# Block-sorted attention and a routed expert layer: a fixed order for the attention phase, and another access pattern where mixed k and v leave PSUM

## The chip, the core and the metric

One core of a Trainium2 chip runs the whole program in one launch. Time is device microseconds of one execution. The kernel before takes 630.01 us (median of 3 runs, 629.17 to 630.42). Its engines are named as in the profile: PE (TensorE, matmuls), PEld (its weight loads), DVE (VectorE), ACT (ScalarE), POOL (GpSimd) and SP (SyncE, which issues DMAs). POOL and ACT issue DMAs too.

## What is computed

There are 4 x 8 = 32 attention heads with a sequence of 768 rows, cut into 8 blocks of 96, and a head size of 64. A small matrix P (8 x 8 for each head) is normalised five times; it mixes the blocks of k and of v; each block of q then attends to the mixed block at its own place. The result, 3072 rows of 512, goes through a router, which sends each row to one of 8 experts.

```python
P = sort_net
for _ in range(5):
    P = np.exp(P - np.max(P, axis=-1, keepdims=True))
    P = P / (np.sum(P, axis=-1, keepdims=True) + 1e-09)
    P = P / (np.sum(P, axis=-2, keepdims=True) + 1e-09)
k_sorted = np.einsum('bhij,bhjcd->bhicd', P, k_b)
v_sorted = np.einsum('bhij,bhjcd->bhicd', P, v_b)
scores = scale * np.matmul(q_b, k_sb.transpose(0, 1, 2, 4, 3))
attn = softmax(scores)               # over the last axis
x = np.matmul(attn, v_sb)            # then rows of 512
e_idx = np.argmax(x @ w_gate + modality_bias[modality_id], axis=1)
out[mask] = gate_w * (np.maximum(x[mask] @ w1[e], 0.0) @ w2[e])   # for each expert e
```

## The kernel before

The heads are handled in two groups of 16 (`g` = 0, 1). The stages follow one another like this.

- Loads. `load_k(g)` brings k of a group in 6 pieces of 256 KB into a small buffer (`k_raw`, two of them) and spreads each into `k_il`, a zero-filled array in which the two halves of the partitions take alternate columns. `load_v(g)` brings v in one DMA of 1.5 MB into `v_in`. `load_q(g, hq)` brings two heads' q and rearranges it on VectorE into `q_il`. All three issue DMAs from GpSimd's queue, which works in order, as all the queues do.
- Normalisation. Five rounds (lines 119 to 131) of Exp on ScalarE and six short VectorE operations, each waiting for the one before. Lines 133 to 159 make the mixing matrices `bd_k` and `bd_v` out of the result.
- Mixing. A group has 28 jobs, 12 of `sort_k` and 16 of `sort_v`. A job is 8 or 4 matmuls into one PSUM bank (`mipsum`, two slots) and one copy of 512 values per partition from there to SBUF, with conversion to bf16. The copy of `sort_k` goes to `kTb`, where neighbouring values of the copy land 192 bytes apart; that of `sort_v` goes to `v_sb`, where they land 130 bytes apart. Group 0's jobs run before the first unit, alternating between VectorE and ScalarE.
- Units. 32 units, one head of a group and half of its blocks each: `trans_q` (6 transposes on TensorE, one copy on VectorE; only in the first half of a group), `scores` (8 matmuls), `expo` (one Exp on ScalarE), `av` (8 matmuls, then two reciprocals and two multiplications on VectorE, which write `xb`). From u = 2 to 15 two jobs of group 1 are written into each unit, one for each of the two engines. After every eighth unit, SyncE issues 12 DMAs of 64 KB that write `xb` to `x_scratch` in DRAM. There is one `xb`, so the first write of the next block waits for them.
- Between mixing and the units stands the set-up of the router: small constants, a load of `w_gate`, and a DMA that fills `sidx_scratch` with 3968 records of 8 bytes out of a tile (`dummy_t`) that VectorE clears.
- Router. 24 tiles of 128 rows are read back from `x_scratch` (ScalarE's queue), transposed, multiplied with `w_gate`; each ends in a small write to `cnt_scratch` on GpSimd's queue. After the last one `cnt` is read back, a serial chain computes where each row goes, and 24 indirect DMAs scatter the row numbers.
- Experts. 31 slots of 128 rows, each gathered, multiplied with w1 and w2 of one expert, and scattered to the output. The weights of all 8 experts lie in `w_all`, 8192 columns of each partition for one expert; `kTb`, `v_in`, `k_il` and the transposed q occupy the columns of experts 3 to 7 during attention, so those weights can be loaded only when these are done with. `load_weights(e)` is two DMAs of 1 MB each on GpSimd's queue.

The order of the instructions on each engine is not the program's. A scheduler places them by its own cost estimates and by program order as a priority, and it moves what is independent a long way: the set-up of the router runs inside the first 25 us, and weight loads are issued from 27 us on, wherever their columns are free.

Of the kernel before, what the change touches and what calls it, by code (L numbers as in the profile page):

```python
# [17 lines left out]
def kernel(  # L18
# [67 lines left out]
    nc.vector.memset(k_il[0:64, :, 1], 0.0)
    nc.vector.memset(k_il[64:128, :, 0], 0.0)
    load_k(0)
    load_v(0)
    q_tiles = {}  # L90
# [424 lines left out]
```

## Time and profile before

| | us |
|---|---|
| median of 3 runs | 630.01 |
| the profiled execution | 628.43 |
| its span, from the first to the last instruction | 626.3 |
| start to the first copy of a mixed chunk | 50.0 |
| mixing of group 0 | 47.4 |
| units with jobs of group 1 between them | 67.6 |
| the other units, with the writes of x, to the router's first transposes | 68 |
| router | 57.2 |
| routing chain and scatter of the row numbers | 121.8 |
| experts | 214.3 |

[...] Over the span PE is busy 44%, DVE 42%, ACT 31% and POOL 22%: no engine is near full over the whole, so each stage has to be read by itself. In the rows further down, a group of instructions shows its line, engine, operation, the tiles it writes and reads, shapes and count, and behind the bar its busy time, the mean length of one in ns, and the idle time of its engine just before it with what ended it. In a timeline a row begins with its start and its length in us; the square bracket holds the idle time before it and what ended that.

### The profile page before, as it was taken

To read this page: it belongs to the slowest core of one execution; us is meant where nothing else is said; L and a number is where in the kernel's file an instruction comes from. 1 tells how busy PE (TensorE), PEld (TensorE's weight loads), DVE (VectorE), ACT (ScalarE), POOL (GpSimd) and SP (SyncE) were. 2 spreads that over 40 slices of the span, in tenths; PEclk is the share of its full clock that TensorE was granted. 3 is DMA by queue.
4 is the path that set the end of the run, shared out by engine and by line. 5 is a ranking of instruction groups with operands and counts; after the bars stand their busy time and mean duration, and the time that the engine had idled before them with its cause. 6 is when DMAs were issued, how large, how long until landed. Compare 5 with 4: busy or idle time off the path is not lost.

```text
span 626.3 us, 6878 instructions
## 1 busy us (share of the span) xinstructions
PE 277.0 (44%) x2026; PEld 157.8 (25%) x2044; DVE 261.8 (42%) x769; ACT 192.7 (31%) x431; POOL 137.3 (22%) x180
## 2 busy tenths in 40 slices
PE   0002327653754406551000000068787886787775
PEld 0002225542532203331000000023333333333332
DVE  4438888878743506553000000023444343433342
ACT  0006775787332205551000000023333332333222
POOL 5311102110000101222222222122332332223222
PEclk9999999999999999999999999999999998999999
DMA  7999858793826593210000000011121121211210
GB/s 141 119 121 204 140 83 152 117 196 58 136 51 112 83 201 81 59 40 1 7 0 0 0 0 0 0 42 52 51 69 58 50 76 35 68 51 52 46 17 10
DMA packets 41337, 43.56 MB, mean 70 GB/s; under 512 B 14396, under 2 KB 32869, under 8 KB 41046
## 3 DMA queue, kind: packets, MB, share of 16 engines
q0 software_dynamic: 25184, 36.72, 31.6%
q1 hardware_dynamic: 12662, 3.26, 3.4%
q10 hardware_dynamic: 3456, 3.15, 2.2%
q8 instruction: 18, 0.29, 0.2%
q14 instruction: 17, 0.14, 0.1%
HBM read 59.83 MB, written 11.33 MB: 114 GB/s over the span
## 4 chain that ended last, share of the span: by engine, by line
DMA 29%; PE 27%; issue 16%; DVE 15%; ACT 8%; POOL 3%; SPq 1%; POOLq 0%; DVEq 0%; ACTq 0%
DMA sidx_scratch<-rg_all,dest_i_all 12%; PE h_p L462 8%; PE y_p L477 7%; DMA x_scratch<-xb 4%; PE hT_p L473 3%; ACT v_sb L175 3%; DVE v_sb L175 3%; DVE y_sb L481 3%; DMA x_t<-x_scratch,idxg 3%; DVE w_all L168 3%; DMA k_raw<-in_k_dram 3%; DMA q_in<-in_q_dram 2%; ACT w_all L168 2%; DMA out_dram<-y_sb,idxg 2%; PE va L173 2%
## 5 line engine op out<-in xcount | busy, mean ns | idle before, releaser
L456 PE MATMUL xT_p<-ident,x_t 128*128 128x128 bf16 x124 | 21.3, 221 | 141.2 <-DMA x_t<-x_scratch,idxg 123.4
L477 PE MATMUL y_p<-w_all,hT 128*128 x237 | 73.2, 379 | 0.6 <-ACT hT L474 0.6
L457 ACT COPY xT<-xT_p 128x128 bf16<-128x128 bf16 x62 | 16.5, 266 | 167.4 <-PE xT_p L456 167.4
L462 PE MATMUL h_p<-w_all,xT 128*128 x241 | 60.4, 391 | 9.9 <-issue 9.6
L450 POOL DMA_INDIRECT x_t<-x_scratch,idxg x31 | 30.5, 983 | 133.1 <-PE h_p L462 50.9
L457 DVE COPY xT<-xT_p 128x128 bf16<-128x128 bf16 x62 | 11.5, 217 | 111.3 <-PE xT_p L456 111.2
L473 PE MATMUL hT_p<-ident,h_sb 128*128 128x128 bf16 x248 | 49.6, 221 | 10.7 <-DVE hT L474 9.6
L474 DVE COPY hT<-hT_p 128x128 bf16<-128x128 bf16 x124 | 27.9, 225 | 46.6 <-PE hT_p L473 42.0
L456 PEld LDWEIGHTS <-x_t 128*128 128x128 bf16 x124 | 9.8, 97 | 144.1 <-DMA x_t<-x_scratch,idxg 127.0
L175 DVE CAST v_sb<-va 96x512 bf16<-96x512 f32 x16 | 39.1, 2445 | 10.2 <-PE va L173 10.1
L175 ACT CAST v_sb<-va 96x512 bf16<-96x512 f32 x16 | 39.3, 2454 | 12.5 <-PE va L173 12.5
L474 ACT COPY hT<-hT_p 128x128 bf16<-128x128 bf16 x124 | 32.8, 264 | 29.8 <-PE hT_p L473 26.1
L219 ACT ACTIVATE attnT<-sc 96x768 bf16<-96x768 f32 x32 | 26.8, 841 | 48.9 <-PE op L232 39.1
L467 DVE TENSOR_SCALAR h_sb<-h_p 128x512 bf16<-128x512 f32 x31 | 21.4, 692 | 47.5 <-PE h_p L462 47.5
L434 POOL DMA_INDIRECT sidx_scratch<-rg_all,dest_i_all x24 | 23.4, 974 | 75.7 <-DMA sidx_scratch<-rg_all,dest_i_all 71.3
L469 ACT ACTIVATE h_sb<-h_p 128x512 bf16<-128x512 f32 x31 | 18.5, 597 | 63.8 <-PE h_p L462 58.5
L482 POOL DMA_INDIRECT out_dram<-y_sb,idxg x31 | 31.4, 1014 | 25.9 <-DVE xT L457 13.2
L462 PEld LDWEIGHTS <-xT 128*128 128x128 bf16 x248 | 24.7, 99 | 46.3 <-issue 25.7
L168 ACT CAST w_all<-ka 128x512 bf16<-128x512 f32 x12 | 32.5, 2712 | 8.3 <-PE ka L166 8.3
L477 PEld LDWEIGHTS <-hT 128*128 128x128 bf16 x248 | 23.9, 96 | 44.0 <-issue 16.5
L481 DVE TENSOR_SCALAR y_sb<-y_p,idxg 128x512 f32<-128x512 f32 x31 | 23.3, 751 | 27.3 <-PE y_p L477 26.4
L236 DVE TENSOR_TENSOR xb<-op,rs 96x256 bf16<-96x256 f32 x64 | 26.0, 417 | 18.5 <-DMA x_scratch<-xb 16.9
(126 smaller groups left out, 450.4 us busy)
## 6 DMA issues: line engine op xcount, KB each, us to landing
w_all<-in_moe_w_dram POOLq DMA_DIRECT2D x16, 1024.0 KB, 12.2
k_raw<-in_k_dram POOLq DMA_DIRECT2D x12, 256.0 KB, 7.7
w_all<-in_v_dram POOLq DMA_DIRECT2D x2, 1536.0 KB
q_in<-in_q_dram POOLq DMA_DIRECT2D x16, 192.0 KB, 7.5
x_scratch<-xb SPq DMA_DIRECT2D x48, 64.0 KB, 6.1
x_t<-x_scratch ACTq DMA_DIRECT2D x24, 128.0 KB, 2.4
idxg<-sidx_scratch SPq DMA_DIRECT2D x31, 1.0 KB, 1.7
x_t<-x_scratch,idxg POOLq DMA_INDIRECT x31
```

The lines of the kernel that those rows point to most:

```text
L168: (nc.scalar.copy if act else nc.vector.tensor_copy)(dst, acc)
L175: (nc.scalar.copy if act else nc.vector.tensor_copy)(dst, acc[0:BLK])
L219: nc.scalar.activation(attnT[u % 3][:, 0:8 * BLK].rearrange("p (r f) -> p r f", r=2), sc_tiles.pop(u)[0:BLK, :, 0:4 * BLK], ACT.Exp, scale ...
L450: nc.gpsimd.indirect_dma_start(out=x_t, out_offset=None, in_=x_dram, in_offset=bass.IndirectOffsetOnAxis(ap=idx[:, :1], axis=0))
L456: nc.tensor.transpose(xT_p, x_t[:, c * 128:(c + 1) * 128], ident)
L457: (nc.scalar.copy if c % 2 else nc.vector.tensor_copy)(xT[:, c], xT_p)
L462: nc.tensor.matmul(h_p, xT[:, c], w_all[:, bass.ds(e_sv * WCOL + c * F + half * 512, 512)], start=(c == 0), stop=(c == 3))
L473: nc.tensor.transpose(hT_p, h_sb[:, fc * 128:(fc + 1) * 128], ident)
L474: (nc.scalar.copy if fc % 2 else nc.vector.tensor_copy)(hT[:, fc], hT_p)
L477: nc.tensor.matmul(y_p, hT[:, fc], w_all[:, bass.ds(e_sv * WCOL + 4 * F + fc * Dm, Dm)], start=(fc == 0), stop=(fc == 7))
L481: nc.vector.tensor_scalar(y_sb, y_p, gate_t[:, 0:1], None, ALU.mult)
L482: nc.gpsimd.indirect_dma_start(out=out, out_offset=bass.IndirectOffsetOnAxis(ap=idx[:, :1], axis=0), in_=y_sb, in_offset=None, bounds_chec ...
```

## The change

- From the loads to the last unit everything stands inside `tc.manual_schedule()`: each engine executes its instructions in the order in which the program writes them. The program's order is rewritten for that. The normalisation starts behind one memset, with the spreads of k put into its rounds 2 to 4; mixing of group 0 follows; then the set-up of the router; then the units, in each of which `expo(u)`, `scores(u + 1)`, `prep_q(u + 2)`, two jobs and `av(u)` follow one another.
- The copies of mixed chunks walk the chunk the other way round: the source in PSUM is read with a stride of 256 bytes (k) or 512 bytes (v), and the destination in SBUF is written in runs of 8 values (16 bytes) or 4 values (8 bytes). `v_sb` has rows of 72 values, not 65.
- All jobs of group 1 copy on ScalarE; those of group 0 still alternate.
- k of a group comes in 3 DMAs of 512 KB, straight into the space of `v_sb[1]`; one half of the partitions is spread by VectorE, the other by GpSimd. Some memsets move to GpSimd.
- `xb` lies in the columns of expert 2, one for each half of a group. Therefore the weights of experts 2 to 7 are loaded behind attention; those of experts 0 and 1 at u = 14 and 19 (before: 0, 1 and 2 at u = 14, 18 and 22).

```diff
...
-    KCH = 6
+    KCH = 3
-    def load_k(g):
-        for kc in range(KCH):
-            raw = apool.tile([128, KCW * D], BF16, tag="k_raw", name=f"k_raw{g}_{kc}", bufs=2)
-            nc.gpsimd.dma_start(out=raw, in_=k_src[g * 128:(g + 1) * 128, kc * KCW * D:(kc + 1) * KCW * D])
-            rv = raw.rearrange("p (c d) -> p c d", d=D)
-            for par in range(2):
-                rows = slice(par * 64, (par + 1) * 64)
-                nc.vector.tensor_copy(k_il[rows, kc * KCW:(kc + 1) * KCW, par], rv[rows])
...
-    apool = ph1.enter_context(tc.tile_pool(name="apool", bufs=3))
+    apool = ph1.enter_context(tc.tile_pool(name="apool", bufs=2))
...
+    order = ExitStack()
+    order.enter_context(tc.manual_schedule())
...
+    v_sb = [a1.tile([128, 128, VW], BF16, tag=f"v_sb{gg}", name=f"v_sb{gg}") for gg in range(2)]
+    k_raw = v_sb[1].rearrange("p x d -> p (x d)")[:, 0:BLK * D]
...
+    def load_k(g):
+        for kc in range(KCH):
+            cs = slice(kc * KCW * D, (kc + 1) * KCW * D)
+            nc.gpsimd.dma_start(out=k_raw[:, cs], in_=k_src[g * 128:(g + 1) * 128, cs])
+
+    def spread_k(kc, par):
+        rows = slice(par * 64, (par + 1) * 64)
+        cs = slice(kc * KCW * D, (kc + 1) * KCW * D)
+        eng = nc.gpsimd if par else nc.vector
+        eng.tensor_copy(k_il[rows, kc * KCW:(kc + 1) * KCW, par],
+                        k_raw[rows, cs].rearrange("p (c d) -> p c d", d=D))
...
+    def spread_q(g, hq):
+        t = q_raw.pop((g, hq))
+        il = apool.tile([128, 2, 6, 2, D], BF16, tag="q_il", name=f"q_il{g}_{hq}")
         for z in range(2):
             nc.vector.tensor_copy(il[:, z], t[:, :, z].rearrange("p r (t d) -> p t r d", d=D))
         q_tiles[g, hq] = il
...
+    nc.vector.memset(k_il[0:64, :, 1], 0.0)
+    make_identity(nc, ident)
+    load_k(0)
+    load_v(0)
     load_q(0, 0)
     load_q(0, 1)
-
-    nc.vector.memset(v_in[:, BLK * D:128 * D], 0.0)
-    v_sb = [a1.tile([128, 128, D + 1], BF16, tag=f"v_sb{gg}", name=f"v_sb{gg}") for gg in range(2)]
-    for gg in range(2):
-        nc.gpsimd.memset(v_sb[gg][:, :, D:D + 1], 1.0)
-    attnT = [a1.tile([96, 8 * BLK + 32], BF16, tag=f"attnT{z}", name=f"attnT{z}") for z in range(3)]
+    nc.gpsimd.memset(k_il[64:128, :, 0], 0.0)
+    nc.gpsimd.memset(v_in[:, BLK * D:128 * D], 0.0)
+    for kc in range(KCH):
+        spread_k(kc, 1)
+    nc.gpsimd.memset(v_sb[0][:, :, D:D + 1], 1.0)
     for z in range(3):
         nc.gpsimd.memset(attnT[z][:, 8 * BLK:], 0.0)
...
     for it in range(5):
         if it == 0:
             nc.vector.tensor_reduce(red, P_t, AX.X, ALU.max)
             nc.vector.tensor_tensor(P_t, P_t, red.broadcast_to([BH, NB, NB]), ALU.subtract)
         nc.scalar.activation(P_t, P_t, ACT.Exp)
+        if it == 0:
+            nc.vector.tensor_reduce(jmask, id3s, AX.X, ALU.add)
+        elif it == 1:
+            nc.vector.tensor_reduce(bmask, id3, AX.X, ALU.add)
+            for g in range(2):
+                nc.vector.tensor_copy(sel[g], ident[0:BH, g * 16:(g + 1) * 16].broadcast_to([BH, 16, NB]))
+        else:
+            spread_k(it - 2, 0)
         nc.vector.tensor_reduce(red, P_t, AX.X, ALU.add)
         nc.vector.reciprocal(red, red)
         nc.vector.tensor_tensor(P_t, P_t, red.broadcast_to([BH, NB, NB]), ALU.mult)
...
+    make_bd(0)
...
-        dst = kTb[g].rearrange("p (x c) -> p c x", c=BLK)[:, ch * 8:(ch + 1) * 8]
-        (nc.scalar.copy if act else nc.vector.tensor_copy)(dst, acc)
+        src = acc.rearrange("p z x -> p x z")
+        dst = kTb[g].rearrange("p (x c) -> p x c", c=BLK)[:, :, ch * 8:(ch + 1) * 8]
+        (nc.scalar.copy if act else nc.vector.tensor_copy)(dst, src)
...
-        dst = v_sb[g].rearrange("p x d -> p d x")[0:BLK, ch * 4:(ch + 1) * 4]
-        (nc.scalar.copy if act else nc.vector.tensor_copy)(dst, acc[0:BLK])
...
+        src = acc[0:BLK].rearrange("p z x -> p x z")
+        dst = v_sb[g][0:BLK, :, ch * 4:(ch + 1) * 4]
+        (nc.scalar.copy if act else nc.vector.tensor_copy)(dst, src)
...
     for n, (f, g, ch) in enumerate(sort_jobs[0]):
         f(g, ch, n % 2)
+        if n == 11:
+            load_k(1)
+            make_bd(1)
+    load_v(1)
+    load_q(0, 2)
+    load_q(0, 3)
...
-            x_tiles[g, hf] = apool.tile([BLK, 2, 4, H, D], BF16, tag="xb", name=f"xb{g}_{hf}", bufs=1)
+            x0 = 2 * WCOL + hf * 8 * Dm
+            x_tiles[g, hf] = w_all[0:BLK, x0:x0 + 8 * Dm].rearrange("p (r i h d) -> p r i h d", r=2, i=4, h=H)
...
-    WLOAD = {14: 0, 18: 1, 22: 2}
+    WLOAD = {14: 0, 19: 1}
...
-    load_q(0, 2)
-    load_q(0, 3)
-    trans_q(0, 0)
+    def prep_q(u):
+        if u < 32 and (u // 8) % 2 == 0:
+            if u % 2 == 0:
+                spread_q(u // 16, (u % 8) // 2)
+            trans_q(u // 16, u % 8)
+
+    prep_q(0)
+    prep_q(1)
     scores(0)
     pend = list(sort_jobs[1])
     for u in range(32):
-        if u == 0:
-            load_k(1)
-            load_v(1)
+        if u < 3:
+            spread_k(u, 1)
+            spread_k(u, 0)
+        if u == 3:
+            nc.gpsimd.memset(v_sb[1][:, :, D:D + 1], 1.0)
         if 9 <= u <= 12:
             load_q(1, u - 9)
         if u in WLOAD:
             load_weights(WLOAD[u])
         expo(u)
-        n = u + 1
-        if n < 32:
-            if (n // 8) % 2 == 0:
-                trans_q(n // 16, n % 8)
-            scores(n)
-        av(u)
-        if u >= 2 and u < 16:
+        if u + 1 < 32:
+            scores(u + 1)
+        prep_q(u + 2)
+        if u >= 2:
             for z in range(2):
                 if pend:
                     f, g, ch = pend.pop(0)
-                    f(g, ch, z)
+                    f(g, ch, 1)
+        av(u)
+    order.close()
     ph1.close()
-    for e in range(3, E):
+    for e in range(2, E):
         load_weights(e)
```

## Rows read from the trace of the kernel before

**Rows 1.** Busy time by stage: us, PE, PEld, DVE, ACT, POOL (instructions); PEclk; DMA share, GB/s
```profile
0.00:50.00 50.00, 0.90 (x15) 0.84 (x16) 21.98 (x68) 2.56 (x6) 16.72 (x35) 1.00 0.99 132
50.00:97.40 47.40, 14.58 (x159) 12.45 (x157) 40.75 (x27) 35.95 (x14) 5.45 (x9) 1.00 0.80 132
97.40:165.00 67.60, 39.49 (x444) 31.59 (x442) 55.13 (x80) 44.37 (x27) 10.63 (x14) 1.00 0.81 137
```

**Rows 2.** Chain that ended last, first 50 us: start us, us, what
```profile
24.73 15.69 DMA k_raw<-in_k_dram
```

**Rows 3.** Timeline of the start: start us, us, engine, line, operation, tiles, idle before
```profile
0.25 0.10 POOL L499 MEMSET const-float32-0.0<- 128x1 f32 x1 [0.25 <-issue]
7.13 0.30 POOL masks.py:197 MEMSET ident<- 128x128 bf16 x1
7.63 2.07 DVE L71 COPY w_all<-k_raw 64x1024 bf16<-64x1024 bf16 x4 [0.27 <-DMA k_raw<-in_k_dram]
46.17 0.26 ACT L123 ACTIVATE P_t<-P_t 32x64 f32<-32x64 f32 x1 [1.50 <-DVE P_t L131]
49.12 0.31 DVE L157 TENSOR_TENSOR bdk<-bdv 128x64 bf16<-128x64 bf16 x2
```

**Rows 4.** Groups by line and form, 0 to 300 us: busy us, mean ns, idle
```profile
L175 DVE CAST v_sb<-va 96x512 bf16<-96x512 f32 x16 | 39.1, 2445 | 10.2 <-PE va L173 10.1
L168 ACT CAST w_all<-ka 128x512 bf16<-128x512 f32 x12 | 32.5, 2712 | 8.3 <-PE ka L166 8.3
L236 DVE TENSOR_TENSOR xb<-op,rs 96x256 bf16<-96x256 f32 x64 | 26.0, 417 | 18.5 <-DMA x_scratch<-xb 16.9
L127 DVE TENSOR_REDUCE red<-P_t 32x8 f32<-32x64 f32 x5 | 1.3, 253 | 0.2
L124 DVE TENSOR_REDUCE red<-P_t 32x8 f32<-32x64 f32 x5 | 1.0, 207 | 1.3 <-ACT P_t L123 1.3
```

**Rows 5.** Costliest groups of the page: busy us, mean ns, idle before
```profile
L467 DVE TENSOR_SCALAR h_sb<-h_p 128x512 bf16<-128x512 f32 x31 | 21.4, 692 | 47.5 <-PE h_p L462 47.5
L469 ACT ACTIVATE h_sb<-h_p 128x512 bf16<-128x512 f32 x31 | 18.5, 597 | 63.8 <-PE h_p L462 58.5
```

**Rows 6.** Timeline, TensorE in the first mixing stage
```profile
52.77 1.01 PE L166 MATMUL ka<-bdk,w_all 128*128 128x64 bf16 x16 [2.38 <-DVE w_all L168]
```

**Rows 7.** Busy time, as rows 1, around the 8-byte fill and behind it
```profile
24.00:30.00 6.00, 0.00 (x0) 0.00 (x0) 3.39 (x13) 0.26 (x1) 2.57 (x4) 1.00 0.69 28
40.00:60.00 20.00, 3.32 (x50) 2.83 (x50) 16.77 (x39) 8.92 (x6) 4.71 (x7) 1.00 1.15 205
```

**Rows 8.** DMA issues, whole span: count, KB, median us to landing
```profile
sidx_scratch<-dummy_t SPq DMA_DIRECT2D x1, 31.0 KB, 16.2
```

**Rows 9.** Timeline of the unit loop, TensorE, then ScalarE late in it
```profile
98.25 0.50 PE L213 MATMUL sc<-w_all 64*128 64x96 bf16 x8
98.69 0.82 PE L194 MATMUL tq<-ident,q_il 128*128 128x128 bf16 x6
99.88 0.62 PE L232 MATMUL op<-v_sb,attnT 96*128 96x65 bf16 x8
...
174.72 0.81 ACT L219 ACTIVATE attnT<-sc 96x768 bf16<-96x768 f32 x1 [0.87 <-PE op L232]
176.35 0.81 ACT L219 ACTIVATE attnT<-sc 96x768 bf16<-96x768 f32 x1 [0.83 <-PE op L232]
```

**Rows 10.** Timeline of the issues of x_scratch writes, blocks 2 and 4
```profile
174.25 6.22 SPq L244 DMA_DIRECT2D x_scratch<-xb  x12
...
215.49 8.74 SPq L244 DMA_DIRECT2D x_scratch<-xb  x12
```

**Rows 11.** Chain that ended last: the router's first reload
```profile
230.44 2.68 DMA x_t<-x_scratch
```

**Rows 12.** Timeline, GpSimd at the end of the router
```profile
287.97 0.50 POOL L367 DMA_DIRECT2D cnt_scratch<-cnt_sb  x1 [1.38 <-ACT cnt_sb L366]
290.19 0.53 POOL L370 DMA_DIRECT2D cnt<-cnt_scratch  x1 [1.72 <-DMA cnt_scratch<-cnt_sb]
```

More of the change, by code (lines that the diff above doesn't have):

```diff
@@ L82, with load_v @@
     mipsum = ph1.enter_context(tc.psum_pool(name="mipsum", bufs=2))
+    order = ExitStack()
+    order.enter_context(tc.manual_schedule())
+    v_sb = [a1.tile([128, 128, VW], BF16, tag=f"v_sb{gg}", name=f"v_sb{gg}") for gg in range(2)]
+    k_raw = v_sb[1].rearrange("p x d -> p (x d)")[:, 0:BLK * D]
+    attnT = [a1.tile([96, 8 * BLK + 32], BF16, tag=f"attnT{z}", name=f"attnT{z}") for z in range(3)]
+    ident = singles.tile([128, 128], BF16)
     P_t = singles.tile([BH, NB, NB], FP32)
     nc.sync.dma_start(out=P_t, in_=sort_net.rearrange("b h i j -> (b h) i j"))
[L86 to L90, printed above, removed]
+    def load_k(g):
[8 more added lines that the diff above has]
+                        k_raw[rows, cs].rearrange("p (c d) -> p c d", d=D))
+    def load_v(g):
+        nc.gpsimd.dma_start(out=v_in[:, 0:BLK * D], in_=v_src[g * 128:(g + 1) * 128])
+    q_raw, q_tiles = {}, {}
     def load_q(g, hq):
-        t = apool.tile([128, 2, 2, 6 * D], BF16, tag="q_in", name=f"q_in{g}_{hq}", bufs=2)
+        t = apool.tile([128, 2, 2, 6 * D], BF16, tag="q_in", name=f"q_in{g}_{hq}")
         for par in range(2):
@@ L100, in load_q @@
         q_tiles[g, hq] = il
+    nc.vector.memset(k_il[0:64, :, 1], 0.0)
+    make_identity(nc, ident)
+    load_k(0)
+    load_v(0)
     load_q(0, 0)
     load_q(0, 1)
[L105 to L109 removed]
+    nc.gpsimd.memset(k_il[64:128, :, 0], 0.0)
[3 more added lines that the diff above has]
+    nc.gpsimd.memset(v_sb[0][:, :, D:D + 1], 1.0)
     for z in range(3):
         nc.gpsimd.memset(attnT[z][:, 8 * BLK:], 0.0)
[L112 to L113 removed]
+    jmask = singles.tile([128, NB], FP32)
+    bmask = singles.tile([128, 16], FP32)
+    sel = [singles.tile([BH, 16, NB], BF16, tag=f"sel{g}", name=f"sel{g}") for g in range(2)]
     red = singles.tile([BH, NB], FP32)
@@ L131, with make_bd @@
         nc.vector.tensor_tensor(P_bf if it == 4 else P_t, P_t, colb, ALU.mult)
-    id3 = ident.rearrange("p (a j) -> p a j", j=NB)
-    id3s = bass.AP(tensor=ident.tensor, offset=ident.offset,
-                   ap=[ident.ap[0], [1, NB], [NB, 16]])
-    jmask = singles.tile([128, NB], FP32)
-    nc.vector.tensor_reduce(jmask, id3s, AX.X, ALU.add)
-    bmask = singles.tile([128, 16], FP32)
-    nc.vector.tensor_reduce(bmask, id3, AX.X, ALU.add)
     bd_v, bd_k = [], []
-    for g in range(2):
-        sel = singles.tile([BH, 16, NB], BF16, tag=f"sel{g}", name=f"sel{g}")
-        nc.vector.tensor_copy(sel, ident[0:BH, g * 16:(g + 1) * 16].broadcast_to([BH, 16, NB]))
+    def make_bd(g):
         rep = mipsum.tile([128, NB, NB], FP32, tag="mi", name=f"rep{g}")
-        nc.tensor.matmul(rep.rearrange("p a b -> p (a b)"), sel.rearrange("p a b -> p (a b)"),
+        nc.tensor.matmul(rep.rearrange("p a b -> p (a b)"), sel[g].rearrange("p a b -> p (a b)"),
                          P_bf.rearrange("p a b -> p (a b)"), start=True, stop=True)
@@ L173, in sort_v @@
             nc.tensor.matmul(acc[:, z], v_cols[:, ch * 4 + z], bd_v[g], start=True, stop=True)
-        dst = v_sb[g].rearrange("p x d -> p d x")[0:BLK, ch * 4:(ch + 1) * 4]
-        (nc.scalar.copy if act else nc.vector.tensor_copy)(dst, acc[0:BLK])
-    sort_jobs = []
-    for g in range(2):
-        jobs = [(sort_k, g, ch) for ch in range(12)] + [(sort_v, g, ch) for ch in range(16)]
-        sort_jobs.append(jobs)
+        src = acc[0:BLK].rearrange("p z x -> p x z")
+        dst = v_sb[g][0:BLK, :, ch * 4:(ch + 1) * 4]
+        (nc.scalar.copy if act else nc.vector.tensor_copy)(dst, src)
+    sort_jobs = [[(sort_k, g, ch) for ch in range(12)] + [(sort_v, g, ch) for ch in range(16)]
+                 for g in range(2)]
     for n, (f, g, ch) in enumerate(sort_jobs[0]):
         f(g, ch, n % 2)
+        if n == 11:
[4 more added lines that the diff above has]
+    load_q(0, 3)
     x_tiles = {}
```

12 lines of the change are left out of this document (6 added, 6 removed).

## Prediction

> **What bounds the kernel now.** I read the busy time by stage first [rows 1], then the chain of waits of each stage, then the groups by line. In no stage of attention is TensorE full: from 50.0 to 97.4 us it works 14.6 us of 47.4 while VectorE and ScalarE are busy 40.8 and 36.0, and from 97.4 to 165 VectorE works 55.1 of 67.6. What fills them is one kind of instruction, the copy of a mixed k or v chunk out of PSUM: 2.71 us for k, 2.45 us for v [rows 4], though a dense copy of the same 512 values takes 0.69 us on VectorE and 0.60 us on ScalarE [rows 5]. The first 50 us are another matter: the chain ends in DMAs, the longest a k piece of 15.7 us [rows 2], and the normalisation of sort_net waits on VectorE behind the copies of k. Later VectorE waits 16.9 us in all before line 236 for writes that still read the only xb [rows 4]. The router, the serial scatter and the experts come after the last write, and nothing in the diff touches them: they move with what precedes them.
>
> **The working, in the profile's own time** (span 626.3 us, execution 628.4 us; the median of the three runs is 630.0, so 1.6 more). I put the changed kernel's milestones on the trace's clock.
>
> *Head.* VectorE now does one memset, and the five normalisation rounds are interleaved with only three spreads. A round takes 0.26 + 1.50 = 1.76 us [rows 3]. Two quarter-megabyte k pieces were spread by 9.7 us [rows 3]; at 205 GB/s [rows 7] the remaining 1.05 MB of the first group needs 5.1 us more, so the third spread can end about 15 and, with the last round and 1.4 us for the mixing matrix, mixing could start near 18 instead of 49.4 [rows 3]. GpSimd may be later: after its issues (some 7 us) it clears 6144 and 2048 elements and copies 2048 for the first third. No GpSimd copy is in the trace. The nearest rows are its memsets: 0.10 us for 1 element, 0.30 for 128 [rows 3], 1.56 ns for each further element, so 9.6 + 3.2 + 3.3 us and a start at 23; with 2.3 ns (0.30 / 128) it is 31, with 4-byte words in the memsets 17. I take 23, as a contiguous copy is nearest to that memset; its other two thirds, 3.3 us each, keep ahead of TensorE. [...]
>
> *One eviction, E.* The new copy writes runs of 8 (k) or 4 (v) values and reads PSUM with a jump at every value. Floor: dense, 0.69 and 0.60 us. A jump at every read is in the trace only in SBUF: line 127 against line 124, 253 - 207 = 46 ns on 64 values, 0.72 ns each [rows 4]; on 512 values that is 0.37 us, so 1.06. If each write run costs what a lone value costs now (2.71 us less 0.69, over 512: 3.9 ns), 64 or 128 runs add 0.25 or 0.5, so 1.6 at most in this reckoning. A gain below the floor is excluded, as no dense copy of this size is faster. I take 1.0, nearest to the jumping read. The upper end stays unknown, since no row reads PSUM so; it can lie at today's 2.45 to 2.71 or over.
>
> *Mixing group 0.* Two PSUM slots; a pair of jobs lasts E plus about 0.68 us (TensorE needs 1.01 us for 16 matmuls, two jobs, and is released by the copy [rows 6]; 2.71 + 0.68 is today's period). 14 pairs x 1.68 = 23.5, plus 1.5 for the second matrix now in the middle: 23 + 25 = 48. Today 97.4.
>
> *The first units and a new stall.* Through prep_q(0), prep_q(1) and the small memsets the first expo starts at 52, and u = 0 and 1 take 5.5 with their spreads: at 57.5 the program order asks for q(0,2). GpSimd issues its load only behind load_v(1), which waits for the last mixing matmul. Right then SyncE issues the fill of sidx_scratch, whose zero tile VectorE writes in its new place after mixing. That one DMA of 8-byte records took 16.2 us to land [rows 8], and in its first six microseconds the DMA engines moved 28 GB/s against 205 later [rows 7]; the k piece of [rows 2] was its victim. So I put 13 us of block behind 49, then 1.57 MB of v and 0.39 MB of q at 205 GB/s, 9.6 us: q(0,2) at 72. TensorE and VectorE stand still for 14 us, because trans_q and spread_q head their queues with everything behind. The cost may be 0 if the transfers share, 16 if they don't at all.
>
> *Units.* TensorE per unit: scores 0.50, transposes 0.82, k job 0.5, av 0.62 [rows 6, 9]. With two jobs it needs 2.2 to 2.9 us. ScalarE now takes both evictions: 0.81 + 2 x 1.0 + 0.3 for gaps, 3.1. In-order coupling considered, 3.2, and 3.9 with transposes: 8 x 3.2 + 6 x 3.9 = 49 for u = 2 to 15. Units 16 to 21 have transposes alone, 2.4 each; the last ten keep the period of 1.63 [rows 9], taken 1.6: 30.4. Two xb in expert 2's columns remove the waits for line 236's writes. Last av: 72 + 49 + 30 = 151.
>
> *What is late next.* Writes of the last block: 12 issues take 6.2 us in a quiet block and 8.7 beside weights [rows 10], so x is out after 8: 159, today 230. The router took from 230.4 to 288.0 [rows 11, 12], which gives 217. But the change loads only experts 0 and 1 inside attention; 12 transfers of 1.05 MB start when xb is out, 12.6 / 205 = 61 us, plus some 10 for the router's 3.1 MB sharing the engines, and the 24 small cnt writes stand behind them in the same GpSimd queue: 159 + 70 + 2 = 231. That is the later. Today the reload of cnt is issued at 290.2 [rows 12]: 59 us earlier. All behind it shifts: 628.4 - 59 = 569; I say **569 us**. If loads of free columns (experts 6, 7) are moved up into attention, up to 14 us less.
>
> **Rivals.** (a) *The blocks do not bite*: the fill shares, and weights move up. Then 57.5 + 49 + 30 + 8 = 144.5 and the router's 57.5 decide: cnt at 204.5, 86 earlier, 542 us. For it: beside weights the issue of the x writes only stretched from 6.2 to 8.7 us [rows 10]. Against: the first six microseconds of the fill [rows 7]. (b) *Eviction gains only half*, E = 1.8: mixing ends at 59, q at 83 (fill 60, block and transfers 23), units 14 x 4.7 = 66, then 30, 8 and 72: 259, 31 earlier, 597 us. ScalarE is then the bound, as it has all of group 1. (c) *The change does not do what it says*, E stays near 2.6: the same sums give 71, 94.5, 183, 213, 221 and 293, hence 631 us, no change, since the better head pays only for ScalarE's doubled load and the late weights. (d) *Strided PSUM reads cost as much as scattered writes do now*: 3.9 ns for each of 512 values on top of a dense copy and of the 8-byte runs, E = 3.4. Mixing ends at 82, q at 105.5, units 14 x 7.9 = 111, reload at 327: 664 us, slower. It decides from E = 2.55, where 42 us per microsecond of E (14 pairs and 28 evictions on ScalarE) have eaten the 59. Against it: the jumping SBUF read costs 0.72 ns, not 3.9.
>
> [...]
>
> **How the numbers follow.** The forecast has 0.50 and its own range is 552 to 582 (E from 0.7 to 1.3, head 17 to 31). (a) 0.20, (b) 0.18, (c) 0.04, (d) 0.05; 0.03 for another stall of the fixed order that eats everything, counted as slower. So faster 0.88, same 0.02 and slower 0.10, with (c) halved between the last two. A measurement here tells 0.2% from no change. The range reaches to (a) and (b): 538 to 604.
>
> **What would show it.** Copies at lines of sort_k and sort_v near 1.0 us; P_bf by 18 and the first mixing matmul by 18 to 31; spread_q of the third pair waiting on a q DMA with the fill in flight; ScalarE, not VectorE, densest in u = 2 to 15; no wait before the first xb write of a block; weights landing after the last router tile and the cnt reload waiting for them; an unchanged length from that reload to the end (336 us). Wrong it would be if eviction is over 2 us, or if the fixed order waits for a DMA I have not placed.

## The result, and the profile after

The changed kernel takes 555.64 us (median of 4 runs, 555.13 to 558.68) where the kernel before, on the same chip, takes 630.21: a ratio of 0.883 [0.880, 0.886]. The profiled execution of after has a span of 553.4 us, before 626.3. The forecast of 569 is 13 us too high and inside its own range of 552 to 582; several of its steps missed by more than that, with both signs.

| Milestone on the trace's clock, us | before | predicted | after |
|---|---|---|---|
| first mixing matmul | 49.4 | 23 | 23.1 |
| mixing of group 0 ends | 97.4 | 48 | 43.1 |
| q(0,2) is there | no such wait | 72 | 57.4 |
| units 2 to 15 done | – | 121 | 90 |
| last division by the row sum | 215.6 | 151 | 122.3 |
| last x write landed | 230.1 | 159 | 144.0 |
| reload of cnt issued | 290.2 | 231 | 216.9 |
| end of the span | 626.3 | 567 | 553.4 |

Attention ends 93 us earlier, but only 73 reach the end: the way from the last division to the reload of cnt grew from 74.6 to 94.6 us.

The first view is the busy time by stage, as [rows 1]: stretch, length, PE, PEld, DVE, ACT, POOL, granted clock, DMA share, GB/s.

```profile
0.00:23.00 23.00, 0.21 (x1) 0.21 (x2) 19.25 (x45) 2.56 (x6) 22.09 (x27) 1.00 0.83 160
23.00:43.00 20.00, 14.37 (x161) 12.49 (x160) 10.67 (x23) 8.14 (x14) 0.46 (x2) 1.00 0.49 93
58.00:90.00 32.00, 26.68 (x405) 23.02 (x404) 18.81 (x63) 23.61 (x40) 7.54 (x10) 0.97 1.21 168
90.00:122.00 32.00, 22.40 (x294) 16.90 (x292) 23.27 (x78) 13.28 (x17) 8.91 (x12) 0.50 1.19 220
122.00:145.00 23.00, 0.12 (x2) 0.12 (x3) 1.05 (x5) 0.00 (x0) 2.06 (x4) 0.50 1.18 231
```

Mixing of group 0 fills 20 us with the matmuls that took 47.4 before. From 122 to 145 next to nothing is computed, while the DMA engines move 231 GB/s. Of the 20 us that are lost behind attention, 5 lie there (17.6 us from the last division to the router's first transposes before, 22.7 after) and 15 in the router (57.0 and 71.9 us).

The groups by line of 23 to 122 us, as [rows 4] (busy us, mean ns, idle before):

```profile
L196 ACT CAST v_sb<-va 96x512 bf16<-96x512 f32 x24 | 13.9, 625 | 9.1 <-PE va L193 9.1
L188 ACT CAST w_all<-ka 128x512 bf16<-128x512 f32 x18 | 10.3, 586 | 23.9 <-PE ka L185 23.7
L196 DVE CAST v_sb<-va 96x512 bf16<-96x512 f32 x8 | 5.5, 686 | 4.8 <-PE va L193 4.8
L188 DVE CAST w_all<-ka 128x512 bf16<-128x512 f32 x6 | 4.2, 692 | 4.1 <-PE ka L185 4.1
L261 DVE TENSOR_TENSOR w_all<-op,rs 96x256 bf16<-96x256 f32 x63 | 26.5, 421 | 2.3
```

The copies out of PSUM went from 2712 and 2445 ns to 0.59 to 0.69 us, the floor of [rows 5] and not above it; and the write to xb (last row) waits for no DMA any more.

The timeline, by contrast, shows where after waits (start us, us, what, idle before and who ended it): behind mixing for q, before the router for the modality ids, in the router for cnt.

```profile
57.42 0.63 DVE L110 COPY q_il<-q_in 128x768 bf16<-128x768 bf16 x2 [4.30 <-DMA q_in<-in_q_dram]
57.84 0.82 PE L218 MATMUL tq<-ident,q_il 128*128 128x128 bf16 x6 [6.79 <-DVE q_il L110]
106.05 0.82 PE L218 MATMUL tq<-ident,q_il 128*128 128x128 bf16 x6 [4.77 <-DVE q_il L110]
144.56 0.22 DVE L357 CAST mod<-modraw 24x128 bf16<-24x128 int32 x1 [21.35 <-DMA modraw<-in_moe_modality_id_dram]
170.75 0.15 ACT L397 COPY cnt_sb<-cnt_p 1x8 f32<-1x8 f32 x1 [7.99 <-DMA cnt_scratch<-cnt_sb]
216.85 0.53 POOL L401 DMA_DIRECT2D cnt<-cnt_scratch  x1 [1.35 <-DMA cnt_scratch<-cnt_sb]
```

The last row answers [rows 12]. From it to the end are 336.5 us, before 336.1.

### The profile page after: what moved, and what is told of

It reads as the page before. It is cut to its first block, busy times and chain, and to the rows that moved or that the text cites. A ratio compares the mean times of both kernels' runs of the same rounds, so it can differ in the third digit from the quotient of the medians.

```text
span 553.4 us, 6871 instructions
## 1 busy us (share of the span) xinstructions
PE 268.7 (49%) x2044; PEld 153.5 (28%) x2044; DVE 199.5 (36%) x735; ACT 143.7 (26%) x445; POOL 153.7 (28%) x182
## 4 chain that ended last, share of the span: by engine, by line
DMA 31%; PE 30%; issue 20%; DVE 12%; POOL 4%; ACT 2%; POOLq 0%; SPq 0%; ACTq 0%; DVEq 0%
DMA sidx_scratch<-rg_all,dest_i_all 14%; PE h_p L493 10%; PE y_p L508 9%; DMA q_in<-in_q_dram 4%; PE hT_p L504 4%; DVE y_sb L512 3%; DMA x_t<-x_scratch,idxg 3%; DMA out_dram<-y_sb,idxg 2%; POOL cnt_scratch L398 2%; DMA x_t<-x_scratch 2%; PE ka L185 2%; PE xT_p L487 1%; DMA v_sb<-in_k_dram 1%; PE va L193 1%; DVE w_all L261 1%
## 5 line engine op out<-in xcount | busy, mean ns | idle before, releaser
L487 PE MATMUL xT_p<-ident,x_t 128*128 128x128 bf16 x124 | 21.2, 221 | 139.8 <-DMA x_t<-x_scratch,idxg 121.9
L508 PE MATMUL y_p<-w_all,hT 128*128 x248 | 75.2, 376 | 0.0
L493 PE MATMUL h_p<-w_all,xT 128*128 x248 | 63.3, 401 | 8.9 <-issue 8.7
L504 PE MATMUL hT_p<-ident,h_sb 128*128 128x128 bf16 x248 | 49.4, 220 | 10.3 <-DVE hT L505 9.6
L465 POOL DMA_INDIRECT sidx_scratch<-rg_all,dest_i_all x24 | 23.3, 973 | 77.1 <-DMA sidx_scratch<-rg_all,dest_i_all 72.9
L498 DVE TENSOR_SCALAR h_sb<-h_p 128x512 bf16<-128x512 f32 x31 | 21.4, 692 | 48.4 <-PE h_p L493 46.8
L371 PE MATMUL xT_p<-ident,x_t 128*128 128x128 bf16 x96 | 19.9, 278 | 27.5 <-ACT xT L372 14.6
L512 DVE TENSOR_SCALAR y_sb<-y_p,idxg 128x512 f32<-128x512 f32 x31 | 23.3, 751 | 27.2 <-PE y_p L508 27.2
L398 POOL DMA_DIRECT2D cnt_scratch<-cnt_sb x24 | 12.1, 504 | 58.0 <-ACT cnt_sb L397 41.0
L261 DVE TENSOR_TENSOR w_all<-op,rs 96x256 bf16<-96x256 f32 x64 | 26.9, 421 | 2.3
L504 PEld LDWEIGHTS <-h_sb 128*128 128x128 bf16 x248 | 20.6, 97 | 15.5 <-DVE h_sb L498 14.4
## 6 DMA issues: line engine op xcount, KB each, us to landing
w_all<-in_v_dram POOLq DMA_DIRECT2D x2, 1536.0 KB, 14.6
```

The lines of the kernel that those rows point to most:

```text
L261: nc.vector.tensor_tensor(xb[:, par, :, h], op[0:BLK, :, 0:D], rs.broadcast_to([BLK, 4, D]), ALU.mult)
L465: nc.gpsimd.indirect_dma_start(out=sidx_dram, out_offset=bass.IndirectOffsetOnAxis(ap=dest_i_all[:, t:t + 1], axis=0), in_=rg_all[:, t], i ...
L487: nc.tensor.transpose(xT_p, x_t[:, c * 128:(c + 1) * 128], ident)
L493: nc.tensor.matmul(h_p, xT[:, c], w_all[:, bass.ds(e_sv * WCOL + c * F + half * 512, 512)], start=(c == 0), stop=(c == 3))
L504: nc.tensor.transpose(hT_p, h_sb[:, fc * 128:(fc + 1) * 128], ident)
L508: nc.tensor.matmul(y_p, hT[:, fc], w_all[:, bass.ds(e_sv * WCOL + 4 * F + fc * Dm, Dm)], start=(fc == 0), stop=(fc == 7))
```

## Experiments

The kernel before took 632.6, 630.8, 631.1 and 630.5 us beside the four groups of runs, so kernels are compared by their ratio to it.

**The order alone**: after, with the copies that write single values; the order, the loads and the second `xb` stay.

```diff
-        src = acc.rearrange("p z x -> p x z")
-        dst = kTb[g].rearrange("p (x c) -> p x c", c=BLK)[:, :, ch * 8:(ch + 1) * 8]
...
+        dst = kTb[g].rearrange("p (x c) -> p c x", c=BLK)[:, ch * 8:(ch + 1) * 8]
...
```

(v likewise.)

> The changed kernel with one part undone: the copies of mixed k and v write lone values to SBUF again (dense PSUM reads); order, loads and xb stay. Theory 1 (the new copy carries the gain, and the fixed order pays only because the copy is short): a copy is back at 2.45 to 2.71 us, group 0's mixing takes 14 x 3.3 = 46 us instead of 20, and in u = 2 to 15 ScalarE, which holds both copies of a unit, needs 0.8 + 2 x 2.6 = 6 us a unit, 85 us instead of 32; the reload of cnt moves from 217 to about 290 and the time is 620 to 640, like the kernel before. Theory 2 (the order carries at least half of the gain): 555 to 595.

Measured 626.1 us, 0.991 [0.988, 0.993]: theory 1. The groups and the stage show why the order is worth so little by itself:

```profile
L194 ACT CAST v_sb<-va 96x512 bf16<-96x512 f32 x24 | 56.5, 2507 | 7.0 <-PE va L192 6.9
L187 ACT CAST w_all<-ka 128x512 bf16<-128x512 f32 x18 | 48.3, 2806 | 18.8 <-PE ka L185 18.6
98.00:192.00 94.00, 47.72 (x586) 36.80 (x582) 37.80 (x128) 75.95 (x51) 13.58 (x17) 1.00 0.71 125
```

Mixing starts at 23.1, 26 us earlier, but ScalarE now evicts all of group 1, at 2.5 to 2.8 us each, and is busy 76 of 94 us; last division at 191.6, reload of cnt at 286.1. Rival (c) was this case (E near 2.6, reload 293, 631 us), so its total was good to 1 per cent.

**The copy alone**: before, with the new copies and the wider rows of v that they need.

```diff
+        src = acc.rearrange("p z x -> p x z")
...
-        dst = kTb[g].rearrange("p (x c) -> p c x", c=BLK)[:, ch * 8:(ch + 1) * 8]
...
+        dst = kTb[g].rearrange("p (x c) -> p x c", c=BLK)[:, :, ch * 8:(ch + 1) * 8]
...
```

> The kernel before with one part of the change alone: the copies read PSUM with a stride and write runs of 8 or 4 values (v_sb in rows of 72); the scheduler's order stays. Theory 1 (the copy is what bounded mixing): group 0's mixing falls from 47 to some 20 us and the 14 units with two jobs from 4.6 to about 2.7 us each, together 50 us less by the first write of block 2; the first 50 us, with their DMA waits, and the waits for the one xb stay; weights that came earlier with slack now come late and give some back: 570 to 590. Theory 2 (the scheduler's order has DMA waits that take the place of the copies): over 600.

Measured 587.7 us, 0.930 [0.927, 0.932]: theory 1. Mixing still starts at 49.7, but the stage of [rows 1] that it fills has TensorE busy 31.3 us in place of 14.6:

```profile
L177 ACT CAST v_sb<-va 96x512 bf16<-96x512 f32 x16 | 9.4, 588 | 15.5 <-PE va L174 15.5
50.00:97.40 47.40, 31.28 (x430) 26.46 (x428) 30.34 (x78) 17.58 (x28) 11.32 (x17) 0.89 1.16 201
```

The two gains, 7.0 and 0.9 per cent, make 7.9; together they give 11.7. The early start pays only once ScalarE can carry the evictions that the order puts on it.

**Shorter write runs**: k in runs of 4 values, v in runs of 2.

```diff
-        src = acc[0:BLK].rearrange("p z x -> p x z")
-        dst = v_sb[g][0:BLK, :, ch * 4:(ch + 1) * 4]
+        src = acc[0:BLK].rearrange("p (a z) x -> p a x z", z=2)
+        dst = v_sb[g][0:BLK, :, ch * 4:(ch + 1) * 4].rearrange("p x (a z) -> p a x z", z=2)
```

> The changed kernel with the mixed k written in runs of 4 values (8 bytes) and the mixed v in runs of 2 (4 bytes), where it writes 8 and 4 (16 and 8 bytes); PSUM is still read with a jump in most steps. Theory A (each write run has a price, about 4 ns as a lone 2-byte value has in the kernel before): the k copy has 128 runs, about 1.1 us, the v copy 256, about 1.5 us, against 0.69 and 0.59 now; mixing 9 us longer and ScalarE's evictions 28 x 0.6 = 17 us more, partly covered: total 570 to 585. Theory B (only lone 2-byte writes are slow, a 4-byte or longer run writes at full pace): 0.69 and 0.59 us as now, total within 2 us of 555.6.

Measured 557.4 us, 0.886 [0.879, 0.892], which the interval can't tell from after: theory B. The groups:

```profile
L196 ACT CAST v_sb<-va 96x512 bf16<-96x512 f32 x24 | 15.6, 724 | 9.2 <-PE va L193 9.2
L188 ACT CAST w_all<-ka 128x512 bf16<-128x512 f32 x18 | 10.4, 590 | 22.6 <-PE ka L185 22.6
L196 DVE CAST v_sb<-va 96x512 bf16<-96x512 f32 x8 | 5.5, 687 | 4.8 <-PE va L193 4.8
```

Runs of 4 bytes cost VectorE nothing (687 ns, 686 in after) and ScalarE 0.1 us for 256 runs (724 ns, 625 in after); a lone 2-byte value costs 3.4 to 4.1 ns more than a dense one (2.45 and 2.71 us against 0.69 and 0.60, over 512).

**The fill early**: `sidx_fill` issued ahead of mixing, with its two memsets.

> The changed kernel with the fill of sidx_scratch (3968 records of 8 bytes on SyncE's queue) issued ahead of the mixing, at some 23 us, while the DMA engines are idle, in place of 43.1 us beside v of group 1 and q(0,2); nothing is left out. In the changed kernel q(0,2) lands at 57.3 us and VectorE's third pair of q spreads waits 4.3 us for it. Theory 1 (the prediction's block: the small records hold v and q back): v and q, 1.96 MB at some 200 GB/s from 43.1, land at about 53 and the wait goes; last attention unit 3 to 5 us earlier, total 2 to 5 us less than the changed kernel, near 552. Theory 2 (one record of the fill goes for one large packet, so it takes almost nothing from them; the wait is only the 1.96 MB): q(0,2) lands within 1.5 us of 57.3, total within 2 us of 555.6.

Measured 558.2 us, 0.884 [0.878, 0.889]. With the fill issued at 23.3 in place of 43.1, the waiting spread of q(0,2) starts at 56.7 in place of 57.4:

```profile
23.31 0.40 SPq L205 DMA_DIRECT2D sidx_scratch<-dummy_t  x1
56.66 1.03 DVE L110 COPY q_il<-q_in 128x768 bf16<-128x768 bf16 x2 [3.75 <-DMA q_in<-in_q_dram]
```

Theory 2: the wait stays when the fill is out of its way, and the fill adds 0.7 us. From 43 to 58 us after's DMA engines move 153 GB/s, 2.3 MB, about what v and the two pairs of q issued behind it make (1.57 and twice 0.39 MB). In after's trace each 2 us from 47 to 51 see 32 or 33 packets of the fill (8 bytes) and as many of v (12,288 bytes).

**One xb**: `x0 = 2 * WCOL` for both halves of every block.

> The changed kernel with one place for x of a block in place of two that alternate; nothing is left out. The first xb write of blocks 2 to 4 has to wait until the 12 writes of the block before have read it. Theory 1 (prediction: the second place removes real waits): the 12 issues take 6.2 to 8.7 us and land 4.8 to 5.2 us later, so VectorE waits 8 to 11 us at each of three blocks, of which a unit or so is covered: 15 to 25 us more, 571 to 581. Theory 2 (the end is set by the weights that land at 165 and by the cnt writes behind them, not by attention): the waits appear but the tail gives most of it back, 0 to 6 us more, 556 to 562.

Measured 575.6 us, 0.911 [0.906, 0.916]: in theory 1's range, some 18 us more than after by the ratios (2.8 per cent of before). VectorE waits 33.5 us in all, up to 8.0 at once (first row). But the edit does a second thing: it leaves half of expert 2's columns free from the start, and a weight load of 1 MB moves ahead of k (second row):

```profile
L261 DVE TENSOR_TENSOR w_all<-op,rs 96x256 bf16<-96x256 f32 x64 | 26.9, 421 | 35.5 <-DMA x_scratch<-w_all 33.5
1.32 1.09 POOL L280 DMA_DIRECT2D w_all<-in_moe_w_dram  x1 [0.37 <-issue]
```

Mixing starts at 29.3 us, 6.2 late, the last division is at 157.6, 35 late, and the reload of cnt at 237.0, 20 late. So the 18 us are the price of this edit and not of the waits alone; how much of them the late start has, no run here shows.

**The tail: ids early, cnt on SyncE's queue.** One edit each.

```diff
+    nc.sync.dma_start(out=modraw, in_=mod_words)
...
-    nc.sync.dma_start(out=modraw, in_=mod_words)
```

> The changed kernel with the modality words loaded at the start, behind the two bias loads, and not behind the last writes of x on SyncE's queue. Theory 1 (the router's first tile waits for that one DMA, which was issued at 138.6 and landed at 144.5, although the reload of its first three x tiles was issued at 123): the first tile starts near 130, the reload of cnt comes 8 to 15 us earlier, 540 to 548. Theory 2 (weights in flight hold back the x reloads and the cnt writes anyway, and the last x write lands at 144): less than 4 us, 552 to 557.

```diff
-        nc.gpsimd.dma_start(out=cnt_dram[t:t + 1], in_=cnt_sb)
+        nc.sync.dma_start(out=cnt_dram[t:t + 1], in_=cnt_sb)
```

> The changed kernel with the 24 cnt writes and the reload of cnt on SyncE's queue instead of GpSimd's, where they stand behind the weights. Theory 1 (ScalarE stands 8 us at a cnt copy because the buffer's DMA is queued behind 1 MB weight transfers; between two cnt writes lie 13.4 us): the gap goes, reload of cnt 8 to 12 us earlier, 544 to 549. Theory 2 (the x reloads, 5 to 7 us each while weights flow, take its place as the wait): less than 4 us.

Measured 551.4 us, 0.871 [0.867, 0.874], and 550.7, 0.872 [0.868, 0.875]: both between their theories. The reload comes at 209.4 and 208.9, 7.5 and 7.9 us earlier. With early ids the router starts 15 us sooner (129.5) and then loses 12.2 in one wait, as three buffers of cnt_sb are queued behind weights:

```profile
134.53 0.56 POOL L398 DMA_DIRECT2D cnt_scratch<-cnt_sb  x1 [10.96 <-ACT xT L372]
159.70 0.15 ACT L397 COPY cnt_sb<-cnt_p 1x8 f32<-1x8 f32 x1 [12.17 <-DMA cnt_scratch<-cnt_sb]
```

**Both.**

> The two single changes of the tail together: the modality ids are loaded at the start, and the 24 cnt writes and their reload are issued on SyncE's queue, away from the weights. Apart they gave 1.2 and 1.1 per cent: with the ids early the router began at 131 in place of 144.9 us, but the third cnt write landed only at 159.6 behind the weights and the reload came at 209.4; with cnt on SyncE's queue the gap of 13 us went and the reload came at 208.9 (216.9 in the changed kernel). Theory 1 (two waits in series, each hidden by the other): together more than the sum, the router runs from 131 at 2.3 to 2.7 us a tile while weights land, reload at 190 to 198, 19 to 27 us less than the changed kernel, 529 to 537. Theory 2 (the shared DMA traffic sets the router's end, x rows and weights together to about 165 and the remaining tiles after that): no more than the larger of the two or their sum, reload at 201 to 209, 541 to 548.

Measured 545.4 us, 0.865 [0.860, 0.870], reload at 204.6: theory 2's time. Neither wait was simply hidden by the other: SyncE issues the last x writes before the first cnt write, and these wait for row loads of the router, 25.6 us in all, so that the first cnt goes out at 156.0 though it was computed at 134.8, and ScalarE waits 10.6 us for its buffers again.

```profile
SPq L269 <- DMA x_t<-x_scratch: 25.6, 8, 6.7
155.95 5.92 SPq L397 DMA_DIRECT2D cnt_scratch<-cnt_sb  x5
160.78 0.15 ACT L396 COPY cnt_sb<-cnt_p 1x8 f32<-1x8 f32 x1 [10.58 <-DMA cnt_scratch<-cnt_sb]
```

(First row of the waits of 110 to 160 us: total, times, longest.)

**Weights held back** until the x writes have read xb, on top of both.

```diff
-    order.close()
-    ph1.close()
     for e in range(2, E):
         load_weights(e)
+    order.close()
+    ph1.close()
```

> As e8_mod_cnt (modality ids early, cnt on SyncE's queue: 545.4 us, reload of cnt at 204.6), but the loads of experts 2 to 7 keep their place in the written order, behind attention; the first of them needs the columns of x and so waits until the last x writes have read them, where in e8 and in the changed kernel they run from 63 us on beside attention. Nothing is left out. Theory 1 (weights beside them cost the x writes 14 us of landing and each x row load 3 to 4 us, and that is on the path): x lands at about 131, the router starts with free DMA engines, reload at 190 to 198, 531 to 538. Theory 2 (the traffic is only moved: 12.6 MB at some 205 GB/s then run from 131 to 192 beside the router, whose row loads take 5 to 7 us all that time): reload at 203 to 212, 544 to 552.

Measured 543.6 us, 0.862 [0.859, 0.865], which can't be told from both edits alone. The reload comes at 195.8, as theory 1 has it, yet nothing arrives at the end: the small transfers behind the reload are issued behind the loads in GpSimd's queue, and there comes a wait of 8.2 us where after has 0.8:

```profile
203.00 0.53 POOL L436 DMA_DIRECT2D slote_scratch<-se_i  x1
211.74 0.52 POOL L441 DMA_DIRECT2D padbc<-padT_scratch  x1 [8.22 <-DMA padT_scratch<-padT_sb]
```

So in three kernels a wait came where small transfers were issued behind weights (16.8 MB in all) in one queue: 8.0 us in after, 12.2 with early ids, 8.2 here; that the third came from the loads was not shown. How much of the 14 us that the x writes landed late is contention and how much the waits for row loads stays open: in this run x's last write was issued at 143.4, earlier than with both edits alone (155.2) but later than in after (137.6).

**Four q buffers.**

```diff
-        t = apool.tile([128, 2, 2, 6 * D], BF16, tag="q_in", name=f"q_in{g}_{hq}")
+        t = apool.tile([128, 2, 2, 6 * D], BF16, tag="q_in", name=f"q_in{g}_{hq}", bufs=4)
...
     load_q(0, 1)
+    load_q(0, 2)
+    load_q(0, 3)
...
```

> The changed kernel with four buffers for a loaded q pair in place of two, so that q(0,2) and q(0,3) are loaded at the start and the four pairs of group 1 from u = 5 to 8; nothing is left out. In the changed kernel TensorE waits 6.7 us for q(0,2) behind v at 50 to 57 us, and 4.8 us for q(1,3) behind weights at 101 to 106. Theory 1 (the path runs through attention, so every wait taken out of it comes off the end): last attention unit 8 to 11 us earlier, total 8 to 11 us less than the changed kernel, 545 to 548. Theory 2 (the DMA traffic of weights, landing to 165, and the waits of the tail behind it set the end): attention ends 8 to 11 us earlier, but the reload of cnt (216.9 now) comes less than 4 us earlier, total 552 to 556.

Measured 563.7 us, 0.894 [0.891, 0.897], slower than after, which neither theory had. The timeline of the start names the reason: the four more loads stand ahead of GpSimd's clears, and each waits until an earlier load has landed.

```profile
9.52 0.71 POOL L102 DMA_DIRECT2D q_in<-in_q_dram  x1 [2.76 <-DMA v_sb<-in_k_dram]
21.73 0.70 POOL L102 DMA_DIRECT2D q_in<-in_q_dram  x1 [6.55 <-DMA w_all<-in_v_dram]
22.48 5.21 POOL L121 MEMSET w_all<- 64x6144 bf16 x1
31.56 1.03 PE L187 MATMUL ka<-bdk,w_all 128*128 128x64 bf16 x16 [15.04 <-POOL w_all L91]
```

Mixing starts at 31.6, 8.5 late. The waits for q are gone and 6 us of that are won back by the end of attention (124.6). The rest is not, and the reload comes 5 us late, at 222.0, as the last weights do.

**Four q buffers and early weights, on top of both tail edits** (expert 0's weights behind k of group 1 during mixing, expert 1's at u = 2).

> As e8_mod_cnt, with the four q buffers of e9 and with the weights of expert 0 loaded behind k of group 1 during mixing (23 to 42 us, when the DMA engines moved 62 to 66 GB/s in two of the slices) and those of expert 1 at u = 2; nothing is left out. Theory 1 (attention's q waits and the traffic of weights beside the last x writes are both on the path): attention ends 8 to 11 us earlier, the last weights land near 147 in place of 167, reload of cnt at 180 to 190, 520 to 531. Theory 2 (x writes and router rows share with whatever weights are still under way, so only the shorter attention counts): reload at 193 to 198, 534 to 539. Theory 3 (v and q of the next units wait behind expert 0): a new wait of up to 10 us at 50 to 60 us, reload at 200 or later.

Measured 546.4 us, 0.864 [0.860, 0.868], reload at 203.2: no gain over the tail edits, as the same late start stands against it. Theory 1 is not tested by it.

**All of it, mended**: the q loads behind the spreads, and one write for the counts of all tiles.

```diff
-        nc.scalar.copy(cnt_sb, cnt_p)
-        nc.gpsimd.dma_start(out=cnt_dram[t:t + 1], in_=cnt_sb)
+        nc.scalar.copy(cnt_all[:, t], cnt_p)
...
             load_k(1)
+            load_q(0, 2)
+            load_q(0, 3)
+            load_weights(0)
...
```

> What the runs point to, in one kernel: the modality ids loaded at the start; the counts of all 24 tiles kept in one tile and written with one DMA, so that no cnt write stands in a queue and ScalarE no longer waits for their buffers (8.0 us in the changed kernel, 10.6 in e8_mod_cnt); q(0,2) and q(0,3) loaded behind k of group 1 during mixing into four q buffers, behind GpSimd's clears and spreads and not ahead of them as in e9 (mixing began at 31.6 there in place of 23.1); expert 0's weights behind them, expert 1's at u = 9, the rest as before. Nothing is left out. Theory 1 (these waits are in series): mixing starts at 23, no wait for q at 50 to 57 and 101 to 106, last attention unit at 112 to 117, reload of cnt at 178 to 188, total 515 to 527. Theory 2 (x writes, x row loads and weights share the DMA engines and that traffic sets the router's pace): attention ends earlier but the reload comes at 190 to 200, total 527 to 538.

Measured 529.8 us, 0.840 [0.837, 0.842], the fastest kernel here, 26 us (4.3 per cent of before) ahead of the changed one. Mixing starts at 23.1, the last division is at 115.0, the reload at 188.8: theory 1 for attention, between the two for the reload, theory 2's time for the whole. (The profiled execution is the slowest of the six, 534.1 us; from its reload to the end are 343.5 us.) What is left of the router's waits is for x rows:

```profile
115.00:145.00 30.00, 10.41 (x80) 6.03 (x81) 10.60 (x75) 8.50 (x44) 1.40 (x3) 0.50 1.16 232
L370 PE MATMUL xT_p<-ident,x_t 128*128 128x128 bf16 x96 | 19.3, 283 | 31.5 <-DMA x_t<-x_scratch 18.7 <-ACT xT L371 6.9 <-DVE xT L371 3.3
```

## Why the prediction was right, and where its steps failed

*What bounds it.* Right: the copies and the start. By the ratios the copy alone gives 44 us, the rest of the change alone 6, both 74.

*Head.* 23 predicted, 23.1 measured, by another way. GpSimd was earlier than taken (clears 5.23 and 2.23 us for 9.6 and 3.2, spreads 2.16 each for 3.3). P_bf came at 21.5 and not at 18, because VectorE was slowed by GpSimd (below), and the mixing matrix was the last to come.

*One eviction.* Taken 1.0 us, measured 0.69 and 0.59. The terms for the jumping read (0.37) and for the write runs (0.25 to 0.5) are both nothing: only the lone 2-byte write was slow (2.45 and 2.71 us), as the run with shorter runs shows (0.59 to 0.72 us). Rival (d) falls with it.

*Mixing.* 25 us predicted, 20.0 measured: 14 pairs at 1.37 us, E plus 0.68 as reckoned.

*The stall at q(0,2).* The wait is real and at the place named, but 4.3 us on VectorE and 6.8 on TensorE instead of 14. q(0,2) landed at 57.3 us, behind v at 54.0; on each queue all landings that the two traces tell come in the order of the issues (62 of GpSimd's, 63 of SyncE's and 19 of ScalarE's in before; 59, 62 and 19 in after). The step that failed is the block of 13 us: a transfer's own time to landing (16.2 us, [rows 8]) was read as time taken from others. In after as many packets of v as of the fill were moved beside each other (32 or 33 of each in 2 us, from 47 to 51 us). In before the reading of [rows 7] had some ground all the same: the k piece issued at 24.73, 0.7 us behind the fill, has no packet in the trace until 30.6, and the packets of k that start from there to 34 last 2.7 us on the mean, against 0.18 from 42 to 46. In after v was issued ahead of the fill. Whether that order makes the difference, or something else held k back, no run here shows.

*Units 2 to 15.* 49 us predicted, 32 measured. ScalarE was to be the densest engine. It is in the plain units (10.3 of the 11.6 us from 76.3 to 87.9, TensorE 9.6), but not over the whole of u = 2 to 15, where TensorE is busy 26.7 of 32 us and ScalarE 23.6. The period of a plain unit is 1.65 us and not 3.1 to 3.2: an exp of 0.83 and two copies of 0.6, whose rows overlap, with no gaps. The term for the copies and gaps was 2 x 1.0 + 0.3. Two stretches of the units, columns as above, the second late in group 1:

```profile
76.30:87.90 11.60, 9.62 (x152) 8.06 (x152) 7.63 (x28) 10.29 (x20) 2.16 (x3) 1.00 1.17 229
111.00:122.00 11.00, 10.08 (x136) 6.56 (x132) 9.93 (x37) 6.45 (x8) 2.56 (x4) 0.50 1.17 223
```

*Units 16 to 31.* 30.4 predicted, 32 measured, with a wait of 4.8 us for q(1,3) behind weights in the same queue. That is a step that was not in the sum: the loads that stand behind the ordered block in the text were moved up into it, from 63.5 us on, where the prediction had them start when x is out. It had priced such a move only as a gain of up to 14 us.

*What is late next.* This is the step that failed most; that the sum came out near here is luck, as the errors cancelled. x was to be out 8 us after attention and took 22. Before itself takes 14.5 [rows 11]: the sum had the 12 issues and left out the landing of the last write, 6.2 us in before. In after the issues alone take 14 us, beside weights at 231 GB/s and with waits of SyncE for the router's row loads; how the two share this is open. From there to the reload 72 us were predicted and 72.9 measured, but not for the reason given: the last weights landed at about 170, some 46 us before the reload (the 165 in the expectations is the landing of the load before). It was the router, started late by the ids (21 us of VectorE's wait), slowed by row loads of 5 to 7 us beside weights (2.4 to 2.7 behind them) and stopped by cnt writes behind weights (8 us on ScalarE). The three runs on the tail show these waits by taking them out, though in each another wait took a part of the place; the mended kernel, without the ids' and the cnt's, reloads 28 us earlier, of which 7 come from attention.

*xb.* The second place was to remove the 16.9 us of [rows 4]; with one place after has 33.5 us of such waits and takes 18 us more in total, an unmeasured part of it from the late start that came with the edit.

*After the reload.* 336.5 us, unchanged as predicted.

## What to carry to other kernels

Look at what the writes of a copy out of PSUM look like before its length: turned so that 8 bytes or more lie together it ran at the dense pace here (0.59 to 0.69 us, where lone values took 2.45 and 2.71), with 4 bytes within 0.1 us of it, though it read PSUM with a jump. When an early stage becomes that much faster, list the transfers of the next stage by queue: here the ids, behind the x writes on SyncE's queue, and the counts, behind weights on GpSimd's, became the new waits (21.4 and 8.0 us), and with one taken out the next one bit (7.5 and 7.9 us gained at the reload singly, 12.2 together). A load added to an engine's list stands ahead of that engine's own work there (with four q buffers mixing started 8.5 us late), and an edit that frees space can bring one there unasked, as with one xb (6.2 us late).
